# Linear attention and a two-level MoE on one core: a PSUM bank for the kv products, early rows turned by TensorE, and a new order of the steps

## The chip, the core and the metric

One core of a Trainium2 chip. Its engines run their own instruction streams: TensorE (PE; its weight loads are PEld), VectorE (DVE), ScalarE (ACT), GpSimd (POOL) and SyncE (SP, which here only issues DMAs). The metric is the device time of one execution in microseconds; the median of the runs counts.

## What is computed

Linear attention without softmax for 8 batches, 8 heads, 576 tokens and head size 64, an RMS norm over each head, then a mixture of experts: each of the 4,608 tokens picks one of 4 groups and one of 4 experts in it, and goes through that expert alone.

```python
kv  = einsum('bhsd,bhse->bhde', k, v)
out = einsum('bhsd,bhde->bhse', q, kv)
x   = out / sqrt(mean(out * out, -1) + 1e-6) * g_norm      # rows of 512 per token
g   = argmax(x @ w_group);  g_w = softmax(x @ w_group)[g]
e   = argmax(x @ w_expert[g]);  e_w = softmax(x @ w_expert[g])[e]
y   = g_w * e_w * (relu(x @ w1[g, e]) @ w2[g, e])
```

## The kernel before, in words

**Two phases.** The first does attention, routing and the sorting of the tokens by expert; the second runs the experts, one region of sorted rows after the other, the fullest first.

**Attention.** For each batch b, `kv_product` (L489, tiles `kps`) multiplies k and v, four products of two heads each. A chain of links makes `kvx` of it, kv beside kv times the router's weights: `kv_keep` copies it out of PSUM, `kv_transpose` turns it (L500, `tps`), `kvt_keep` copies (L504), `router_product` (L509, `eps_`), `router_keep`. All of them write the PSUM pool `ps_k`, which has one bank. Then `o_product` (L535, `ops`) gives a tile of 128 tokens, attention and logits in one product. There are 36 tiles: four for each batch, and one for the tails of each pair. For each tile `o_keep` (L540) copies to a ring `xo`, `logits_keep` copies the logits (`xr`), `squares` squares on ScalarE, or on POOL where SQUARE says G, and `mean_squares` sums on VectorE (L563, `ms`).

**Routing.** Tiles are routed in groups, GS = 7, 6, 6, 5, 6, 6. `route` finds for each token its expert and its weight on VectorE (L653 to L827), with a count over tokens on TensorE (L736 to L742, `rk`); `keys` (L768) are the rows in a DRAM buffer `xs`. There each pair of experts shares a stack that grows from the middle to both sides. For each tile POOL writes the factors (L835) and ids (L839) beside the rows and scatters them (`put_rows`, L244). After group PICK the fullest expert so far is picked (the star). After group EARLY, that is 24 tiles, its 256 outermost rows (HEAD) are read back by `early_region`: four DMAs by quarters of a row (L264) and one for the ids (L267). `scale_rows` (L281), `turn_x` (DVE transposes, L271) and ScalarE bring them into shape, and `early_products` puts them through the star's weights (L309, L313). This fills TensorE while the last group is routed. Then `order_regions` sorts the experts by count (`eidx`, `srow`).

**Order.** The steps of the first phase are not in the order of the code. Each `step` names an engine, a cost, the steps that it needs and a rank. `give_out` simulates the engines with these costs and emits the steps in the order that comes out; ties go by rank. The ranks (RANK, ROUTE, FOLD, LOADS, QLOADS, KVS) and costs are tables of numbers. Where the simulated TensorE would idle, `keep_warm` puts dummy products (L383, `warm`), one for each FILL = 0.28 us.

**Second phase.** `read(0)` reads the 128 rows of region 0 by quarters and `read(1)` those of region 1; after that SP loads the first full expert's weights (`load_weights`, L202). Region 0 goes through the star's weights in one piece (L309, L1367, L313). The last early product is cut in two (CUT), and region 0 is scaled and turned on VectorE between its halves. From region 1 on every product is done three times with split operands (L320, L321, L325), which holds TensorE for the rest of the time. Results are scattered to the output by POOL.

Of the kernel before, what the change touches and what calls it, by code (L numbers as in the profile page):

```python
# [24 lines left out]
GS = [7, 6, 6, 5, 6, 6]  # L25
XO = 20
XR = 18
QUICK = [0, 1, 2, 3, 4, 5]
# [3 lines left out]
EARLY = 3  # L32
# [3 lines left out]
RANK = {'ek': 1033.97, 'o': -457.88, 'ok': 58.4, 'sq': -33.02, 'red': -2582.62, 'w': -3332.77, 'wl': 4032.68, 'wl2': 4.61, 'xt': -3333.23, 'xs': -16.12, 'l1': -24.14, 'hs': -2608.76, 'l2': -2582.04, 'lk': -1004.47}  # L36
ROUTE = [-3190.17, 201.83, -3534.26, -636.71, 2427.37, -1191.6]
FOLD = [-6173.1, 4817.84, -3763.76, -4043.25, 6157.36, -6.99]
LOADS = [-9663.18, -8528.25, -2577.24, -29.38, 7.48, 419.99, 2424.36, 2902.19]
QLOADS = [-7229.2, -996.03, 2.08, -798.29, 41.64, 9.14, 962.0, 1915.11]  # L40
KVS = [-52.25, -5002.75, -4908.62, 59.57, -908.96, -793.37, 845.7, 4.08]
KEEP = 'DDAAAAAA'
SQUARE = 'AAGAAGAAGAAGAAGAAGAAGAAGA' + 'A' * 11
LOGITS = 'A' * 36
FILL = 0.28


SAME = {"PE": 0.0, "A": 0.14, "D": 0.14, "G": 0.1, "S": 0.0}
OTHER = {"PE": 0.2, "A": 0.16, "D": 0.18, "G": 0.1, "R": 0.0, "W": 1.2}
# [4 lines left out]
CUT = 5  # L54

@with_exitstack
def tile_linattn_moe(ctx: ExitStack, tc: tile.TileContext, qm, qt, k, v, router, w1, w2, out):
# [146 lines left out]

    def load_weights(expert):
        ev = expert_index(expert)
        parts = []
        for (wv, rows, cols) in ((w1v, DM, FF // 2), (w2v, FF, DM // 2)):
            for hf in range(2):
                t, d = load_half(ev, wv, rows, cols, hf)  # L210
                parts.append([t, None, None])
        return parts[0:2], parts[2:4]
# [43 lines left out]
    def read_quarters(x, row, n, eng, head=False):  # L256
        for i in range(4):
            cols = slice(REC * i, REC * (i + 1))
            for lo, hi in ((0, n // 32), (n // 32, n // 32 + 1)):
# [4 lines left out]
                got_rows(eng.dma_start(x[32 * i:32 * i + m, lo:hi, :], src.rearrange("(g t) f -> t g f", t=m)), head)  # L264

# [75 lines left out]
    sid = cp.tile([P, 2], I32, name="sid")  # L341
# [6 lines left out]
    with ExitStack() as ph:  # L348
# [4 lines left out]
        ps_e = ph.enter_context(tc.tile_pool(name="ps_e", bufs=2, space=bass.MemoryType.PSUM))  # L353
# [143 lines left out]
        def kv_transpose(b):  # L497
            kv["ps"] = ps_k.tile([P, 512], F32, name="tps", tag="psk")
            for pr in range(NP):
                nc.tensor.transpose(kv["ps"][:, pr * P:(pr + 1) * P], kvx[b % 4][:, pr, NR:NR + P], ident)  # L500

        def kvt_keep(b):
            kv["t"] = ap_.tile([P, 512], F32, name="kvt", bufs=1)
            nc.scalar.copy(out=kv["t"], in_=kv["ps"])  # L504
# [678 lines left out]
    with ExitStack() as ph:  # L1183
# [80 lines left out]
        def read(r):  # L1264
            row = first_row(srow[0:1, r:r + 1])
            read_quarters(xqs[r % 2], row, CAPS[r], nc.sync)
            if r == 0:
                read_ids(rid, row, 1, nc.sync)
# [316 lines left out]
```

## Time and profile before

| | us |
|---|---|
| median of 3 runs (565.05 to 567.49) | 566.06 |
| the profiled execution | 572.79 |
| its span, first to last instruction | 571.1 |
| PE busy in the span | 550.4 (96%) |
| DVE / ACT / POOL busy | 393.3 / 264.7 / 279.2 |
| HBM read and written | 106.04 MB and 20.58 MB |

Busy times are of the span. A busy TensorE isn't one that does useful work: the fillers count as busy too. In a timeline each row is a run of equal instructions: start, us, engine, line, operation, tiles and shapes; in brackets the idle time of the engine ahead of it and what ended that. In a view by windows each engine has its busy time and, in parentheses, its instructions; then come the granted clock of TensorE (1.00 is 2.4 GHz), the busy share of the DMA engines and GB/s.

### The profile page before, as it was taken

To read this page: it belongs to the slowest core of one execution; us is meant where nothing else is said; L and a number is where in the kernel's file an instruction comes from. 1 tells how busy PE (TensorE), PEld (TensorE's weight loads), DVE (VectorE), ACT (ScalarE), POOL (GpSimd) and SP (SyncE) were. 2 spreads that over 40 slices of the span, in tenths; PEclk is the share of its full clock that TensorE was granted. 3 is DMA by queue.
4 is the path that set the end of the run, shared out by engine and by line. 5 is a ranking of instruction groups with operands and counts; after the bars stand their busy time and mean duration, and the time that the engine had idled before them with its cause. 6 is when DMAs were issued, how large, how long until landed. Compare 5 with 4: busy or idle time off the path is not lost. (4 is left out here: it accounts for less than half of the span.)

```text
span 571.1 us, 11636 instructions
## 1 busy us (share of the span) xinstructions
PE 550.4 (96%) x4257; PEld 515.6 (90%) x4257; DVE 393.3 (69%) x777; ACT 264.7 (46%) x475; POOL 279.2 (49%) x314
## 2 busy tenths in 40 slices
PE   7999989999999999999999999999999997999995
PEld 3788877688599999999999999999999997999995
DVE  2347998861488677786768686777868785767760
ACT  0356665631355353445453544545454644455450
POOL 5012888463221381838383827355473834255181
PEclk9999999999999999999999999999999998999999
DMA  8999999435996545463846465564837473653010
GB/s 265 374 418 366 420 410 417 134 138 169 345 331 241 186 157 196 143 234 84 315 147 258 158 243 192 200 244 147 302 92 307 146 269 120 254 207 142 10 36 32
DMA packets 46126, 126.29 MB, mean 221 GB/s; under 512 B 7413, under 2 KB 28905, under 8 KB 35060
## 3 DMA queue, kind: packets, MB, share of 16 engines
q1 hardware_dynamic: 38132, 106.01, 51.6%
q0 software_dynamic: 7792, 19.48, 9.1%
q8 instruction: 34, 0.56, 0.4%
q10 hardware_dynamic: 144, 0.04, 0.1%
q14 instruction: 24, 0.20, 0.1%
HBM read 106.04 MB, written 20.58 MB: 222 GB/s over the span
## 5 line engine op out<-in xcount | busy, mean ns | idle before, releaser
L1305 POOL DMA_INDIRECT out_dram<-z,idx x141 | 168.5, 1195 | 177.8 <-DVE idx L1278 139.1
L320 PE MATMUL ps<-xh,whi 128*128 128x364 f32 (+14 forms) x480 | 144.1, 300 | 0.0
L325 PE MATMUL ps<-xh,wlo 128*128 128x364 f32 (+14 forms) x480 | 143.9, 300 | 0.0
L321 PE MATMUL ps<-xl,whi 128*128 128x364 f32 (+14 forms) x480 | 143.8, 299 | 0.0
L325 PE MATMUL psy<-hh,w2l 128*128 128x364 f32 (+13 forms) x448 | 136.0, 304 | 2.8 <-DVE w2l L298 2.2
L320 PE MATMUL psy<-hh,w2h 128*128 128x364 f32 (+13 forms) x448 | 135.7, 303 | 1.9 <-issue 1.9
L321 PE MATMUL psy<-hl,w2h 128*128 128x364 f32 (+13 forms) x448 | 136.1, 304 | 0.0
L228 DVE TENSOR_TENSOR wlo<-wr,whi 128x1024 fp32r<-128x1024 f32 x60 | 92.4, 1541 | 24.9 <-ACT whi L224 19.3
L284 ACT ACTIVATE hh<-ps 128x364 fp32r<-128x364 f32 (+14 forms) x120 | 50.3, 420 | 88.8 <-PE ps L325 66.3
L320 PEld LDWEIGHTS ps<-xh,whi 128*128 128x128 f32 x480 | 90.6, 189 | 0.0
L321 PEld LDWEIGHTS ps<-xl,whi 128*128 128x128 f32 x480 | 90.5, 189 | 0.0
L325 PEld LDWEIGHTS ps<-xh,wlo 128*128 128x128 f32 x480 | 90.5, 189 | 0.0
L325 PEld LDWEIGHTS psy<-hh,w2l 128*128 128x128 f32 x448 | 85.2, 190 | 3.9 <-DVE w2l L298 2.8
L320 PEld LDWEIGHTS psy<-hh,w2h 128*128 128x128 f32 x448 | 85.1, 190 | 2.2 <-issue 2.2
L298 DVE TENSOR_TENSOR w2l<-wr,w2h 128x1024 fp32r<-128x1024 f32 x60 | 74.6, 1243 | 17.5 <-ACT w2h L294 10.9
L321 PEld LDWEIGHTS psy<-hl,w2h 128*128 128x128 f32 x448 | 85.1, 190 | 0.3 <-DVE hl L285 0.2
L294 ACT CAST w2h<-wr 128x1024 fp32r<-128x1024 f32 x60 | 62.6, 1043 | 46.0 <-PE psy L321 46.0
L285 DVE SCALAR_TENSOR_TENSOR hl<-ps,hh 128x364 fp32r<-128x364 f32 (+14 forms) x120 | 55.5, 464 | 34.6 <-ACT hh L284 28.3
L1292 ACT ACTIVATE xh<-xt,rw 128x364 fp32r<-128x364 f32 (+14 forms) x60 | 32.7, 545 | 71.3 <-DVE xt L271 70.0
L224 ACT CAST whi<-wr 128x1024 fp32r<-128x1024 f32 x60 | 62.2, 1036 | 0.0
L281 POOL TENSOR_TENSOR xq<-xq 128x1280 f32<-128x1280 f32 (+4 forms) x15 | 35.5, 2367 | 22.3 <-DMA xq<-xs 22.2
L244 POOL DMA_INDIRECT xs<-xo,keys x36 | 38.0, 1056 | 13.2 <-POOL xo L839 7.1
(254 smaller groups left out, 653.5 us busy)
## 6 DMA issues: line engine op xcount, KB each, us to landing
wr<-in_w_dram SPq DMA_DIRECT2D x64, 1024.0 KB
m_q<-in_qm_dram SPq DMA_DIRECT2D x8, 1024.0 KB
m_k<-in_k_dram SPq DMA_DIRECT2D x7, 1024.0 KB
m_v<-in_v_dram SPq DMA_DIRECT2D x7, 1024.0 KB
xq<-xs SPq DMA_DIRECT2D x28, 136.0 KB
xq<-xs SPq DMA_DIRECT2D x20, 153.0 KB
out_dram<-z,idx POOLq DMA_INDIRECT x141
xq<-xs SPq DMA_DIRECT2D x8, 187.0 KB
```

The costliest lines, as they stand in the source:

```text
L224: nc.scalar.copy(out=hi, in_=w)
L228: eng.tensor_tensor(out=lo, in0=w, in1=hi.bitcast(F32), op=ALU.subtract)
L244: sc = nc.gpsimd.indirect_dma_start(out=xs, out_offset=bass.IndirectOffsetOnAxis(ap=keys[:, c:c + 1], axis=0), in_=x.rearrange("p i f -> p ...
L281: eng.tensor_tensor(out=part(x, n), in0=part(x, n), in1=factors(x, n), op=ALU.mult)
L284: nc.scalar.activation(out=hh, in_=ps, func=AF.Relu)
L285: nc.vector.scalar_tensor_tensor(out=hl, in0=ps, scalar=0.0, in1=hh.bitcast(F32), op0=ALU.max, op1=ALU.subtract)
L294: nc.scalar.copy(out=piece(hi, hf, i2), in_=halfpiece(wt[hf][0], i2))
L298: nc.vector.tensor_tensor(out=piece(lo, hf, i2), in0=halfpiece(wt[hf][0], i2), in1=piece(hi, hf, i2).bitcast(F32), op=ALU.subtract)
L320: nc.tensor.matmul(ps, lhsT=stat_h(c), rhs=mov_h(c), start=(c == 0), stop=False)
L321: nc.tensor.matmul(ps, lhsT=stat_h(c), rhs=mov_l(c), start=False, stop=False)
L325: nc.tensor.matmul(ps, lhsT=stat_l(d), rhs=mov_h(d), start=False, stop=(d == n - 1))
L1305: sc = nc.gpsimd.indirect_dma_start(out=out4, out_offset=bass.IndirectOffsetOnAxis(ap=idx[:, g:g + 1], axis=0), in_=z[:, g, :], in_offset= ...
```

## The change

- `kv_product` keeps the bank of `ps_k`; the other links of the chain and `rv` get a bank of their own, `ps_t`. `ps_e` falls from two banks to one, and the early products alternate between `ps_k` and `ps_e`.
- The star's rows, and those of region 0, are read whole, a token to a partition, by one DMA each (`read_tokens`), ids with them. `scale_tokens` scales and sorts the columns on VectorE, TensorE transposes, ScalarE copies out with the norm's gain. CUT is gone.
- The factors are written for a whole group by two VectorE operations; between two scatters POOL writes ids only. All squares are ScalarE's.
- The weighted logits lie with heads innermost (`pt`, `xr`).
- The two halves of w1 of the first full expert are loaded in the first phase (`next_weights`), w2 after `read(1)`.
- 7 groups, GS = 6, 5, 5, 4, 4, 6, 6; EARLY = 4 (again 24 tiles). Costs and ranks are new, so the order is too.

```diff
-GS = [7, 6, 6, 5, 6, 6]
+GS = [6, 5, 5, 4, 4, 6, 6]
-EARLY = 3
+EARLY = 4
-RANK = {'ek': 1033.97, 'o': -457.88, 'ok': 58.4, 'sq': -33.02, 'red': -2582.62, 'w': -3332.77, 'wl': 4032.68, 'wl2': 4.61, 'xt': -3333.23, 'xs': -16.12, 'l1': -24.14, 'hs': -2608.76, 'l2': -2582.04, 'lk': -1004.47}
+RANK = {'wn': 87.54, 'ek': -4236.76, 'o': 8245.9, 'ok': 5.78, 'sq': 116.73, 'red': 1698.88, 'w': -9.4, 'wl': 4910.9, 'wl2': -108.2, 'xt': -1910.07, 'xs': -38.32, 'l1': 16.82, 'hs': -2762.23, 'l2': 33.79, 'lk': -29.78}
...
-SQUARE = 'AAGAAGAAGAAGAAGAAGAAGAAGA' + 'A' * 11
+SQUARE = 'AAAAAAAAAAAAAAAAAAAAAAAAAAAAAAAAAAAA'
...
-OTHER = {"PE": 0.2, "A": 0.16, "D": 0.18, "G": 0.1, "R": 0.0, "W": 1.2}
+OTHER = {"PE": 0.2, "A": 0.27, "D": 0.18, "G": 0.1, "R": 0.0, "W": 1.2}
...
+    def read_tokens(x, row, nb, eng, head=False):
+        got_rows(eng.dma_start(x.rearrange("p j i f -> p j (i f)"),
+                               xs[bass.ds(row, P * nb), :].rearrange("(j p) f -> p j f", p=P)), head)
+
+    def scale_tokens(out, x):
+        nc.vector.tensor_tensor(out=out.rearrange("p (r i x) -> p i r x", r=4, i=4), in0=part(x, 4), in1=factors(x, 4),
+                                op=ALU.mult)
...
-        ps_e = ph.enter_context(tc.tile_pool(name="ps_e", bufs=2, space=bass.MemoryType.PSUM))
+        ps_t = ph.enter_context(tc.tile_pool(name="ps_t", bufs=1, space=bass.MemoryType.PSUM))
+        ps_e = ph.enter_context(tc.tile_pool(name="ps_e", bufs=1, space=bass.MemoryType.PSUM))
...
         def kv_transpose(b):
-            kv["ps"] = ps_k.tile([P, 512], F32, name="tps", tag="psk")
+            kv["e"] = ps_t.tile([P, 512], F32, name="tps", tag="pst")
...
         def router_product(b):
-            kv["ps"] = ps_k.tile([P, 512], F32, name="eps_", tag="psk")
+            kv["e"] = ps_t.tile([P, 512], F32, name="eps_", tag="pst")
...
-            xrt[c] = ap_.tile([P, H, NR], F32, name="xr", bufs=XR)
+            xrt[c] = ap_.tile([P, NR, H], F32, name="xr", bufs=XR)
...
+            def f():
+                for lo, hi in [(0, min(nt, XO - r0)), (min(nt, XO - r0), nt)]:
+                    for d in range(2 if hi > lo else 0):
+                        at = (r0 + lo) % XO
+                        eng.tensor_tensor(
+                            out=ring[:, at:at + hi - lo, d::2, FAC:FAC + 4],
+                            in0=v["rinv"][:, lo:hi].rearrange("p t (r h) -> p t h r", h=2),
+                            in1=v["cw"][:, lo:hi].unsqueeze(2).unsqueeze(3).to_broadcast([P, hi - lo, 2, 4]),
+                            op=ALU.mult)
+            w = do(e, nt * 16, [w], f, us=0.4)
+
             def put(c):
-                t = c - c0
-                nc.gpsimd.tensor_scalar(
-                    out=xot[c][:, :, FAC:FAC + 4].rearrange("p (h d) r -> p h d r", h=2),
-                    in0=v["rinv"][:, t, :].rearrange("p (r h) -> p h r", h=2).unsqueeze(2).to_broadcast([P, 2, 2, 4]),
-                    scalar1=v["cw"][:, t:t + 1], scalar2=None, op0=ALU.mult)
                 nc.gpsimd.tensor_copy(out=xot[c][:, :, TOK:REC].bitcast(I32),
...
         def early_region(do, rows):
...
-                row = first_row(star_row)
-                read_quarters(xq0, row, HEAD, nc.sync, head=True)
-                read_ids(sid, row, 2, nc.sync, head=True)
-            s = do("S", 0, rows + [done["star_row"]], f, us=4.7)
+                read_tokens(xq0, first_row(star_row), HEAD // P, nc.sync, head=True)
+            s = do("S", 0, rows + [done["star_row"]], f, us=2.8)
...
+        def next_weights():
+            def f():
+                st["next"] = expert_index(eidx[0:1, 1:2])
+                st["w1n"] = load_layer(st["next"], 0)
+            step("S", 5.1, RANK["wn"], [done["eidx"]], f, take=2)
...
+                    t["tr", j] = early_bank("xtr")
+                    for c in range(KC):
+                        nc.tensor.transpose(t["tr", j][:, c * P:(c + 1) * P], t["t"][:, j * DM + c * P:j * DM + (c + 1) * P],
+                                            ident)
...
-        w1n, w2n = load_weights(eidx[0:1, 1:2])
+        w1n, w2n = st["w1n"], load_layer(st["next"], 1)
...
-        whole2(o, h1, w2c[1], hi=CUT)
-        scale_rows(nc.vector, xqs[0], 4)
+        whole2(o, h1, w2c[1])
+        xn = xt.rearrange("p c t -> p (c t)")
+        scale_tokens(xn, xqs[0])
+        nc.scalar.copy(out=st["ys"][:, 1, DM // 2:DM], in_=o)
+        tp = ps_h.tile([P, 512], F32, name="ps")
         for c in range(KC):
-            turn_x(xt[:, c], xqs[0], 4, c)
-        nc.scalar.activation(out=xT, in_=xt, func=AF.Copy, scale=g2[:, 0:1])
-        whole2(o, h1, w2c[1], lo=CUT)
-        nc.scalar.copy(out=st["ys"][:, 1, DM // 2:DM], in_=o)
+            nc.tensor.transpose(tp[:, c * P:(c + 1) * P], xn[:, c * P:(c + 1) * P], ident)
+        nc.scalar.activation(out=xT, in_=tp.rearrange("p (c t) -> p c t", c=KC), func=AF.Copy, scale=g2[:, 0:1])
```

How the order moves is seen best at two places. The first is TensorE from batch 7's last kv product (`kps`) to its first tiles (`ops`). Before:

```order
L489 MATMUL kps<-tail_v,ktail_173 64x64 x2
...
L383 MATMUL warm<-wide_b,ones_b 128x512
L500 MATMUL tps<-ident,kvx_168 128x128 x4
...
L509 MATMUL eps__1565<-gw,kvt 128x40 x4
...
L535 MATMUL ops<-kvx_168,m_q 128x168 x8
```

and with the change, from the rank products of the group that ends with tile 24:

```order
L750 MATMUL rk<-ohs,upper_b 128x64
L543 MATMUL ops<-kvx_168,m_q 128x168 x4
L497 MATMUL kps<-m_v,m_k 64x64 x8
...
L497 MATMUL kps<-tail_v,ktail_175 64x64 x2
L543 MATMUL ops<-kvx_168,m_q 128x168 x4
L508 MATMUL tps<-ident,kvx_170 128x128 x4
...
L517 MATMUL eps__1554<-gw,kvt 128x40 x4
...
L543 MATMUL ops<-kvx_170,m_q 128x168 x12
```

A tile of the batch before (`kvx_168`) now stands where fillers stood between batch 7's products and their turning; three fillers are left on either side of `eps`.

The second place is SP's queue from the star's weights (`wr`) on. Before:

```order
L202 DMA wr_1348<-in_w_dram 128x2048
...
L202 DMA wr_1581<-in_w_dram 128x2048
L197 TENSOR_LOAD star_row
L264 ISA
L264 DMA xq_180<-xs 32x8x136
...
L267 DMA sid<-xs 128x2x1
L197 TENSOR_LOAD srow
L264 ISA
L264 DMA xq_1956<-xs 32x4x136
```

and with the change:

```order
L203 DMA wr_1567<-in_w_dram 128x2048
L198 TENSOR_LOAD star_row
L267 ISA
L267 DMA xq_182<-xs 128x2x544
...
L203 DMA wr_1767<-in_w_dram 128x2048
L194 TENSOR_LOAD eidx
L203 ISA
L203 DMA wr_1883<-in_w_dram 128x2048
L203 ISA
L203 DMA wr_1885<-in_w_dram 128x2048
L198 TENSOR_LOAD srow
L267 ISA
L267 DMA xq_1942<-xs 128x544
```

Three of the star's four weight loads now stand behind the head rows' read, and the next expert's two loads of w1 ahead of region 0's.

## Rows read from the trace of the kernel before

**Rows 1.** By windows: window and length, then PE, PEld, DVE, ACT, POOL, clock, DMA.
```profile
8.84:110.96 102.12, 95.57 (x1167) 79.85 (x1166) 70.96 (x213) 55.68 (x144) 46.93 (x81) 1.00 0.97 375
110.96:144.37 33.41, 33.27 (x160) 26.72 (x158) 16.58 (x74) 8.73 (x23) 17.10 (x28) 1.00 0.41 139
144.37:160.42 16.05, 15.32 (x57) 9.82 (x57) 8.08 (x12) 5.99 (x10) 3.79 (x2) 1.00 1.00 325
160.42:571.10 410.68, 399.63 (x2858) 396.65 (x2856) 294.31 (x467) 193.00 (x298) 204.14 (x158) 0.99 0.52 186
```
**Rows 2.** By windows, the filler products (`warm`) alone.
```profile
8.84:110.96 102.12, 17.74 (x66) 1.00 0.97 375
110.96:115.07 4.11, 4.11 (x19) 1.00 0.18 72
```
**Rows 3.** Who waited for whom, PE, 0 to 112 us: total, times, longest.
```profile
PE kps L489 <- DMA tail_v<-in_v_dram: 2.0, 3, 0.8
PE kps L489 <- DMA m_v<-in_v_dram: 1.7, 3, 0.8
```
**Rows 4.** Timeline of PE, from batch 7's last kv product to the early products.
```profile
98.08 0.64 PE L489 MATMUL kps<-m_v,m_k 128*64 128x64 f32 x16
98.55 0.29 PE L489 MATMUL kps<-tail_v,ktail 128*64 128x64 f32 x4
...
100.36 0.66 PE L500 MATMUL tps<-ident,kvx 128*128 128x128 f32 x4
...
108.93 0.47 PE L736 MATMUL rk<-carry,ones_f 1*128 1x112 f32 x2
...
109.66 1.36 PE L535 MATMUL ops<-kvx,tail_q 128*64 128x168 f32 x16
110.96 4.28 PE L383 MATMUL warm<-wide_b,ones_b 128*128 128x512 bf16 x19
115.07 8.80 PE L309 MATMUL l<-xx,wr 128*128 128x256 f32 x40
```
**Rows 5.** By windows, as in rows 1: the stretches in which attention's inputs load.
```profile
0.00:8.00 8.00, 5.80 (x19) 2.37 (x20) 3.33 (x12) 1.28 (x1) 7.13 (x46) 1.00 0.72 192
8.00:85.00 77.00, 70.76 (x915) 60.38 (x914) 48.42 (x127) 40.41 (x106) 30.32 (x51) 1.00 1.02 394
```
**Rows 6.** Timeline of POOL: one tile's scatter, the 24th's, and the last.
```profile
90.42 1.05 POOL L244 DMA_INDIRECT xs<-xo,keys  x1 [0.28 <-POOL xo L839]
91.51 0.36 POOL L835 TENSOR_SCALAR xo<-nwy,cw 128x16 f32<-128x16 f32 x1
...
92.30 1.05 POOL L244 DMA_INDIRECT xs<-xo,keys  x1 [0.28 <-POOL xo L839]
...
103.70 1.05 POOL L244 DMA_INDIRECT xs<-xo,keys  x1 [0.28 <-POOL xo L839]
...
132.34 0.97 POOL L244 DMA_INDIRECT xs<-xo,keys  x1 [0.30 <-issue]
```
**Rows 7.** Timeline of SP: the head rows' read, and region 0's.
```profile
106.72 2.35 SPq L264 DMA_DIRECT2D xq<-xs  x4
...
135.57 1.86 SPq L264 DMA_DIRECT2D xq<-xs  x4
```
**Rows 8.** Timeline of DVE: head rows scaled, last group's keys, region 0 scaled.
```profile
111.62 1.23 DVE L281 TENSOR_TENSOR xq<-xq 128x1024 f32<-128x1024 f32 x1 [0.42 <-DMA xq<-xs]
...
124.93 0.25 DVE L768 TENSOR_REDUCE keys<-kr 128x6 int32<-128x96 f32 x1
...
141.82 0.69 DVE L281 TENSOR_TENSOR xq<-xq 128x512 f32<-128x512 f32 x1 [0.35 <-DMA xq<-xs]
```
**Rows 9.** Timeline of ACT: a copy of 512 columns out of PSUM.
```profile
101.05 0.58 ACT L504 COPY kvt<-tps 128x512 f32<-128x512 f32 x1 [0.48 <-PE tps L500]
```
**Rows 10.** By windows, as in rows 1: a stretch of the second phase.
```profile
470.00:480.00 10.00, 6.94 (x54) 6.50 (x53) 4.72 (x7) 3.77 (x8) 8.03 (x7) 1.00 0.16 54
480.00:485.00 5.00, 4.29 (x23) 4.29 (x24) 3.72 (x7) 2.81 (x4) 0.00 (x0) 0.66 0.68 234
```

More of the change, by code (lines that the diff above doesn't have):

```diff
@@ L203, in load_half, with load_layer @@
         return t, d
+    def load_layer(ev, layer):
+        wv, rows, cols = ((w1v, DM, FF // 2), (w2v, FF, DM // 2))[layer]
+        return [[load_half(ev, wv, rows, cols, hf)[0], None, None] for hf in range(2)]
     def load_weights(expert):
         ev = expert_index(expert)
[L207 to L212, printed above, removed]
+        return load_layer(ev, 0), load_layer(ev, 1)
     def quarter(part, h):
@@ L1060, in f @@
                 nc.vector.tensor_copy(out=eidx, in_=v["rv"][0:1, 0:NE])
[L1061 removed]
+            y = done["eidx"] = do("D", 16, [x], f)
             def f():
@@ L1119, in early_products, with early_bank, f @@
             t = {}
-            x, free = [], [None, None]
-            for c in range(KC):
-                def f(c=c):
-                    if c == 0:
-                        t["tx"] = big.tile([P, 2, KC, HEAD], F32, name="xx", tag="w8")
-                        t["t"], t["x"] = t["tx"][:, 0], t["tx"][:, 1]
-                    turn_x(t["t"][:, c], st["xq0"], HEAD // 32, c)
-                s = step("D", 0.35, r0 + RANK["xt"] + 0.1 * c, st["scaled"], f, take=1 if c == 0 else 0)
-                def f(c=c):
-                    nc.scalar.activation(out=t["x"][:, c], in_=t["t"][:, c], func=AF.Copy, scale=g2[:, 0:1])
-                x.append(step("A", 0.35, r0 + RANK["xs"] + 0.1 * c, [s], f))
+            x = []
+            bank = [0]
+            def early_bank(nm):
+                bank[0] += 1
+                return (ps_k, ps_e)[(bank[0] - 1) % 2].tile([P, 512], F32, name=nm, tag=("psk", "pse")[(bank[0] - 1) % 2])
+            free = [done["kk", B - 1], None]
+            for j in range(HEAD // P):
+                def f(j=j):
+                    if j == 0:
+                        t["tx"] = big.tile([P, 2, KC, HEAD], F32, name="xx", tag="w8")
+                        t["t"], t["x"] = t["tx"][:, 0].rearrange("p c t -> p (c t)"), t["tx"][:, 1]
+                    scale_tokens(t["t"][:, j * DM:(j + 1) * DM], st["xq0"][:, j])
+                s = step("D", 0.62, r0 + RANK["xt"] + 0.1 * j, [st["read"]], f, take=1 if j == 0 else 0)
+                def f(j=j):
+                    if j == 1:
+                        st["warm"] = None
+                    t["tr", j] = early_bank("xtr")
+                    for c in range(KC):
+                        nc.tensor.transpose(t["tr", j][:, c * P:(c + 1) * P], t["t"][:, j * DM + c * P:j * DM + (c + 1) * P],
+                                            ident)
+                s = step("PE", 0.62, r0 + RANK["l1"] - 1 + 0.1 * j, [s, free.pop(0)], f)
+                def f(j=j):
+                    nc.scalar.activation(out=t["x"][:, :, j * P:(j + 1) * P],
+                                         in_=t["tr", j].rearrange("p (c t) -> p c t", c=KC), func=AF.Copy,
+                                         scale=g2[:, 0:1])
+                x.append(step("A", 0.59, r0 + RANK["xs"] + 0.1 * j, [s], f))
+                free.append(x[-1])
             hs = []
@@ L1134, in f @@
                 def f(f_=f_):
-                    st["warm"] = None
-                    t["l1", f_] = ps = ps_e.tile([P, 512], F32, name="l1", tag="pse")
+                    t["l1", f_] = ps = early_bank("l1")
                     whole1(ps[:, 0:HEAD], st["ws"][f_ // 4][:, :, f_ % 4 * P:(f_ % 4 + 1) * P], t["x"])
```

100 lines of the change are left out of this document (50 added, 50 removed).

## The prediction

> **What bounds the kernel now.** I read the windows first: they cut the execution where TensorE's work changes [rows 1]. From 160.42 us to the end TensorE is busy 399.63 of 410.68 us with products that this change leaves as they are, so nothing is to be won there. From 110.96 to 160.42 us it is busy too. The room is ahead of 110.96 us, the end of the last attention tile's product: 95.57 of 102.12 us count as busy, but part of that is the `warm` filler. The filler alone stands in the next view [rows 2]: 19 fillers follow each other in 4.11 us, so one takes 0.216 us of TensorE's time. The stretch from 8.84 to 110.96 us holds 64 of them whole (two of the 66 only reach into it), 13.8 us. Real work is 95.57 - 13.8 = 81.8 us, and 6.55 us is idle. Most of that idle time ends with a load of k or v: 2.0 and 1.7 us [rows 3]. The other engines are not full: VectorE is busy 70.96 and ScalarE 55.68 of the 102.12 us [rows 1]. The DMA is: 0.97 of its engines' time there.
>
> Why fillers are there is read from the timeline [rows 4]. The products of batch 7 end at 98.84, then come fillers, the turning of its kv (100.36) and fillers again: TensorE waits for ScalarE and VectorE at each link of the chain from a batch's kv to its first tile. All links of that chain write one PSUM bank, so the next batch's products cannot be put between them.
>
> **The change, part by part.** *Own bank and new order.* In the new order 25 fillers stand between the first kv product and the last tile's product instead of 64, because tiles and kv products of another batch stand between the links. That takes away 39 x 0.216 = 8.4 us. A seventh group adds one more set of rank products, 0.7 us (108.93 to 109.66 [rows 4]). So TensorE's own time says: the attention ends at 8.84 + 81.8 + 5.4 + 0.7 = 96.7 us if no wait is left, and at 103.3 us if all 6.55 us of waits stay. The DMA gives a second floor. Up to 85 us it moves 1.5 + 30.3 = 31.8 MB [rows 5]. The loads up to batch 7's v are 27.0 MB (28.3 MB of inputs less one q and its tail), and some 18 scatters of 0.279 MB stand among them, 5.0 MB. So this v lands at about 85.4 us. Four products of at most 0.76 us (98.08 to 98.84) and the 12.1 us from 98.84 to 110.96, less four fillers that are gone there (0.9 us), end the attention at 99.6 us. The early expert's weights did not compete with this before, as they were issued last; three quarters of them now come behind the head rows. I take 102: the load waits (3.7 us) stay and half of the other 2.8 us too. The ends 96.7 and 103.3 go into the range.
>
> *Head rows* (256 rows of the most wanted expert). These can only be read when the scatters of 24 tiles have landed. POOL is late with them: one tile takes 1.88 us (90.42 to 92.30), and the 24th is out at 104.75 [rows 6]. The factors (0.36 us a tile) go to VectorE as two operations a group, so a tile falls to 1.52 us, and the squares of the tiles up to here leave POOL for ScalarE, which has room [rows 1]. POOL is then not behind when the 24th tile's keys come, just ahead of batch 7's products (say 86.5 us): four tiles end at 92.6, the read starts 1.97 us later as before (106.72 after 104.75 [rows 7]), at 94.6, and lands within the 4.9 us that it took before (VectorE starts at 111.62 [rows 8]), at 99.5 us. That is ahead of 102, so one DMA for five is hidden and counts nothing. If this slack of 2.5 us is gone, the start of the early products slips one for one. The three weight loads behind the read take 2.7 us each at the 394 GB/s of rows 5 and are in by 110 us. The second half of w1 is wanted after four blocks of 1.76 us (five in 8.80 [rows 4]), later than that.
>
> *Early rows turned by TensorE.* Before, 4.11 us passed from the last tile to the early products. Now: 4 fillers (0.9), eight transposes (0.66 for four [rows 4], 1.3), a copy by ScalarE (0.58 [rows 9]) with about 0.1 of handing over: 2.9 us. The early products last as before, 115.07 to 144.37, 29.3 us. Then region 0 is turned by TensorE too, and the filling of that gap with part of the last early product is dropped: 0.66 for the transposes and 0.7 for the copy, in which TensorE stands still. Sum from the last tile to region 0's products: 2.9 + 29.3 + 1.4 = 33.6 us, 0.2 more than the 33.41 of before [rows 1].
>
> *What hides the last group's route.* Counted from the last tile, its keys were done after 14.2 us (125.18), the last scatter after 22.4 (133.31), the first region read started after 24.6 and its rows came after 30.9 (141.82) [rows 6 to 8]. TensorE now wants them, scaled in 0.69, 32.2 us after the last tile. So they are 0.6 us early even without the gain from one DMA for five and from the unit stride of the logits' sum, which I therefore price at nothing. *Two loads of w1* for the next expert now stand ahead of this read on SP's queue. They take 5.3 us and may start while POOL scatters for 8.1 us (125.18 to 133.31). If their slots came late, up to 5.3 us would fall on the read. Between 144.37 and 160.42 us these two loads are gone from a DMA that is at 1.00 there; TensorE idles only 0.73 us in it, so I take nothing.
>
> *The clock.* Through the whole attention the granted clock is 1.00, the 2.4 GHz level, with 6.55 us of idle time in it. Fillers hold TensorE busy while it waits, and most are taken out. The Trainium skill's page TensorE: Matmul & The Clock Gate (What's actually happening) says that "the default state is throttled, and activity releases the throttle", which speaks against taking fillers out. By that rule a stage whose waits are longer than planned would run slow; the trace agrees in so far as no fall is seen where fillers stand, and no run here shows the stage without them.
>
> **Sum.** Attention end 110.96 to 102: -9.0. From there to region 0: +0.2. After it: 0. So -8.8 us. The profiled execution took 572.79 us (span 571.10), 6.7 us over the median of 566.06; TensorE lost time in it at 470 to 485 us (6.94 busy of 10, then a clock of 0.66 [rows 10]), far behind everything that changes. So I take the difference off the median: 557.3 us.
>
> **Rivals.** *Fillers were only a symptom.* Loads or VectorE pace the attention, each filler removed turns into a wait, and its end stays at 111. For it: the DMA share of 0.97. Against it: the bytes, which allow 99.6. Time: 566.06 + 0.2 = 566.3 us.
>
> *Head rows come as late as before.* The attention ends at 102, but POOL or the route holds the read at 106.72; it lands at 109.5 to 111.6, and scaling, turning and copying bring the early products to about 113.2 instead of 115.07. Region 0 costs its 1.4 us more. Time: 566.06 - 1.9 + 1.4 = 565.6 us. For it: the 11 us by which POOL trailed. Against it: 0.36 of 1.88 us a tile is gone.
>
> *The clock falls* (the other side). Where batches 5 to 7 are processed, about 57 to 99 us, 9 fillers are left. If waits for loads grow there and the clock goes to the 1.2 GHz level, work takes twice as long. If half of some 40 us of work runs so: 566.06 - 8.8 + 20 = 577 us. It decides from 8.8 + 2.8 = 11.6 us of such work on. For it: the 0.66 that followed a stretch of 6.94 busy in 10 [rows 10]. Against it: waits of up to 2 us in sum [rows 3] left the clock alone.
>
> **How the numbers follow.** A measurement of this kernel can tell about 0.5%, 2.8 us, from no change. The forecast has a chance of 0.74; with attention ends from 96.7 to 106 it gives 552 to 561 us. Fillers as a symptom: 0.10. Late head rows: 0.08. The clock: 0.08. The first is faster, the middle two are no change, the last is slower. The range reaches from the lower floor to the late head rows, 552 to 566, and leaves out the other two.
>
> **What would show it.** In the changed profile: the last tile's product ending at 100 to 104 us, some 25 fillers ahead of it, POOL's tiles at 1.5 us each, the head read starting ahead of 97 us, the early products less than 4 us behind the last tile, about 1.4 us between the last early product and region 0's, and 33 to 34 us from the last tile to region 0. I am wrong if the attention ends after 107, if a granted clock under 1.00 stands ahead of 150 us, or if region 0 waits for its rows.

## The result and the profile after

The changed kernel took 560.44 us (median of 4 runs, 558.91 to 560.96) beside 566.73 us of the kernel before: a ratio of 0.9889, with a 95% interval from 0.9857 to 0.992. That is 6.3 us less; the forecast was 557.3 us, 8.8 less, with a range of 552 to 566. The profiled execution took 560.28 us. (Ratios leave disturbed runs out and medians do not, so that the two can differ, as in experiment 2.)

By windows, cut at the same places of the program as [rows 1] (columns as there): the attention to the last tile's product, the early products, region 0, the rest.

```profile
9.46:101.63 92.17, 85.82 (x1131) 76.28 (x1130) 62.81 (x245) 60.08 (x155) 29.34 (x48) 1.00 0.97 376
101.63:138.67 37.04, 33.90 (x158) 27.58 (x156) 14.53 (x67) 8.75 (x22) 14.94 (x21) 0.95 0.76 270
138.67:155.20 16.53, 15.31 (x57) 9.82 (x57) 8.08 (x12) 5.72 (x9) 3.78 (x2) 1.00 0.90 279
155.20:558.60 403.40, 396.62 (x2858) 395.05 (x2856) 293.71 (x467) 193.30 (x298) 203.92 (x158) 1.00 0.52 186
```

The attention ends 9.33 us earlier (101.63 for 110.96). The second window is 3.6 us longer, at a mean granted clock of 0.95, and the third 0.5 longer. The rest takes 403.4 us, and 403.3 to 403.9 in the profiles of experiments 5 to 11 and of the control run: so the start of region 1 tells the time of a profiled execution. For the kernel before, 160.42 + 403.6 + 1.7 around the span gives 565.7 us, near its medians of 566.7 here and 565.6 to 566.4 on the second chip of the experiments. Its own profiled execution took some 7 us more for the rest, most of it where the prediction said [rows 10].

The fillers alone, as in [rows 2], in the attention:

```profile
9.46:101.63 92.17, 6.82 (x27) 1.00 0.97 376
```

27 where 66 were (some only reach into the window). Who waited for whom on PE, 9.46 to 165 us (total, times, longest), as in [rows 3]; the first line is one of the kernel before, the others are of the changed kernel:

```profile
PE ops L535 <- DMA m_q<-in_qm_dram: 0.4, 1, 0.4
...
PE ops L543 <- DMA m_q<-in_qm_dram: 2.8, 3, 1.4
PE kps L497 <- DMA m_v<-in_v_dram: 1.9, 3, 1.1
PE kps L497 <- DMA tail_v<-in_v_dram: 1.4, 2, 0.7
PE xtr L1157 <- DVE xx L271: 1.3, 1, 1.3
PE ps L317 <- ACT xT L1386: 0.9, 1, 0.9
PE l L317 <- ACT xx L1162: 0.8, 1, 0.8
```

In the attention, waits for loads make up nearly all idle time: 6.1 of 92.17 - 85.82 = 6.35 us, where they were 4.1 of 6.55 before. New are the waits of the handover, as this text calls the stretch from the last attention tile to the early products. The timeline of PE (as [rows 4]) shows them:

```profile
100.33 1.36 PE L543 MATMUL ops<-kvx,tail_q 128*64 128x168 f32 x16
101.63 1.04 PE L391 MATMUL warm<-wide_b,ones_b 128*128 128x512 bf16 x4
103.92 1.32 PE L1157 MATMUL xtr<-ident,xx 128*128 128x128 f32 x8 [1.25 <-DVE xx L271]
106.02 10.59 PE L317 MATMUL l<-xx,wr 128*128 128x256 f32 x40 [0.78 <-ACT xx L1162]
...
137.13 0.63 PE L1385 MATMUL ps<-ident,xT 128*128 128x128 f32 x4 [0.17 <-PE ps L321]
138.67 0.70 PE L317 MATMUL ps<-wr,xT 128*128 128x512 f32 x1 [0.90 <-ACT xT L1386]
```

From the last tile to the early products 4.39 us pass instead of the 2.9 of the forecast, and the first five blocks take 10.59 us instead of 8.80. The windows show why; the last columns are the granted clock, the DMA share and GB/s:

```profile
101.60:106.00 4.40, 2.35 (x14) 1.15 (x12) 2.76 (x7) 2.87 (x7) 1.83 (x3) 1.00 1.04 428
106.00:108.00 2.00, 1.98 (x5) 1.61 (x6) 1.36 (x6) 0.47 (x2) 1.72 (x3) 0.53 1.07 389
108.00:110.00 2.00, 2.00 (x8) 1.57 (x7) 1.95 (x5) 0.27 (x1) 1.72 (x3) 0.62 1.00 255
110.00:112.00 2.00, 2.00 (x11) 1.77 (x10) 1.77 (x7) 0.50 (x2) 1.50 (x4) 1.00 0.92 351
```

TensorE was busy 2.35 of 4.40 us, then ran for 4 us near the 1.2 GHz level.

Two reads come late, seen on POOL (24th and last scatter) and SP (head read, region 0's), as in [rows 6, 7]:

```profile
93.80 1.00 POOL L244 DMA_INDIRECT xs<-xo,keys  x1 [0.28 <-POOL xo L855]
...
125.08 0.97 POOL L244 DMA_INDIRECT xs<-xo,keys  x1 [0.30 <-issue]
```

```profile
99.40 0.39 SPq L267 DMA_DIRECT2D xq<-xs  x1
100.08 23.22 SPq L203 DMA_DIRECT2D wr<-in_w_dram  x5
133.08 0.33 SPq L267 DMA_DIRECT2D xq<-xs  x1
```

The head read is issued 4.6 us after the 24th scatter left POOL (94.80), and region 0's 7.0 us after the last (126.05). Before, these were 1.97 and 2.3 us [rows 6, 7]. What lies between is in the DMA queues (packets, MB, share of the engines), from 126 to 128, 128 to 130 and 130 to 133 us; hardware_dynamic carries SP's loads, here w1 of the next expert, software_dynamic POOL's scatters:

```profile
q1 hardware_dynamic: 95, 0.65, 88.3%
q0 software_dynamic: 15, 0.07, 7.9%
```

```profile
q1 hardware_dynamic: 70, 0.57, 82.2%
q0 software_dynamic: 66, 0.22, 27.2%
```

```profile
q0 software_dynamic: 159, 0.55, 44.7%
q1 hardware_dynamic: 32, 0.13, 10.8%
```

POOL has issued its last scatter, but while the loads run, little of the scatters moves; most of it comes after 130 us, and only then can the read go out. The Trainium skill's page DMA: Bandwidth & Descriptors (Queues, rings and completion order) says that each DMA engine takes turns between the queues, packet by packet. The 70 and 66 packets from 128 to 130 us agree with it; the 95 and 15 before do not show such turns, and the profile does not tell how many of the scatters' packets were ready then.

**Theory.** The attention is shorter as forecast; 2.5 us of the gain go to loads ahead of two reads in the DMA: the star's first load ahead of the head rows, the next expert's w1 ahead of region 0's. **Rivals.** The reads wait for something else (memory, registers); the clock at the handover is what costs; and, for the gain, bank, fillers or factors.

### The profile page after: what moved, and what is told of

Same layout as the page of the kernel before. It is cut to its first block, busy times and chain, and to the rows that moved or that the text cites. A ratio compares the mean times of both kernels' runs of the same rounds, so it can differ in the third digit from the quotient of the medians.

```text
span 558.6 us, 11537 instructions
## 1 busy us (share of the span) xinstructions
PE 538.9 (96%) x4218; PEld 511.5 (92%) x4218; DVE 382.2 (68%) x803; ACT 269.1 (48%) x484; POOL 259.4 (46%) x276
## 3 DMA queue, kind: packets, MB, share of 16 engines
q1 hardware_dynamic: 36468, 106.01, 53.1%
## 5 line engine op out<-in xcount | busy, mean ns | idle before, releaser
L244 POOL DMA_INDIRECT xs<-xo,keys x36 | 36.1, 1003 | 74.8 <-ACT y L670 41.4
```

What stands on the lines that cost most here:

```text
L244: sc = nc.gpsimd.indirect_dma_start(out=xs, out_offset=bass.IndirectOffsetOnAxis(ap=keys[:, c:c + 1], axis=0), in_=x.rearrange("p i f -> p ...
```

## The experiments

Experiments 1 to 4 ran on one chip, all others on another. Ratios are to the kernel before on the same chip; on the second chip it took 566.43 us beside the control and experiments 5 to 7, and 565.55 beside 8 to 11. Milestones are from one profile each, in us; the attention's end is the last tile product's start plus 1.30. The changed kernel and the control are the same code, and their milestones lie up to 1.6 us apart: so far can two profiles of one kernel differ.

| | attention end | early products | region 0 | region 1 | median | ratio (95%) |
|---|---|---|---|---|---|---|
| before | 110.96 | 115.07 | 144.37 | 160.42 | 566.73 | 1 |
| forecast | 102 | 104.9 | 135.6 | 151.6 | 557.3 | |
| changed | 101.63 | 106.02 | 138.67 | 155.20 | 560.44 | 0.9889 (0.9857 to 0.992) |
| control | 101.30 | 105.46 | 137.08 | 154.21 | 560.2 | 0.9896 (0.9863 to 0.9929) |
| 5 one bank | 102.67 | 110.88 | 141.60 | 157.40 | 563.43 | 0.9953 (0.9927 to 0.9979) |
| 6 no fillers | 103.27 | 106.01 | 137.91 | 155.11 | 558.19 | 0.9871 (0.9831 to 0.9912) |
| 7 factors on POOL | 109.24 | 117.00 | 147.72 | 163.52 | 570.43 | 1.006 (1.0034 to 1.0086) |
| 8 both loads late | 101.26 | 104.02 | 134.77 | 150.57 | 556.36 | 0.9849 (0.9819 to 0.9878) |
| 9 and covered | 101.95 | 105.87 | 137.27 | 153.07 | 555.43 | 0.9815 (0.9789 to 0.9841) |
| 10 one bank, pinned | 101.44 | 105.86 | 136.59 | 155.38 | 559.2 | 0.9883 (0.9855 to 0.9911) |
| 11 head by quarters | 102.47 | 107.39 | 138.13 | 153.94 | 558.2 | 0.9865 (0.9837 to 0.9892) |

**1. The next expert's w1 behind the reads.**

```diff
         early_products(early_weights())
-        next_weights()
...
-        w1n, w2n = st["w1n"], load_layer(st["next"], 1)
+        w1n, w2n = load_weights(eidx[0:1, 1:2])
```

> The changed kernel with one thing undone: the two loads of the next expert's w1 stand behind the reads of regions 0 and 1 on SP's queue again. In the changed kernel the last scatter left POOL at 126.05 us, these loads kept the DMA busy from about 121 to 131.8, and the read of region 0 was issued at 133.08 only. Theory: the scatters land behind those 2 MB. Then the read is issued some 2 us after the last put, near 128, and the rows are there near 131.5. As the early products end at 137 in any case, that is worth 0.2 to 0.5 us: region 0's products at 138.2 to 138.5 instead of 138.67, time -0.5 to 0 us against the changed kernel. Rival: the read waits for memory that the first phase frees (TensorE or ScalarE), not for the scatters; then it stays near 133. Second rival: the loads are needed early; then region 1's first product comes later and the time rises by 1 to 5 us.

**2. The star's first load behind the head read.**

```diff
-                               [wt[-1] if wt else None, done["star_idx"]], f,
+                               [wt[-1] if wt else st["read"], done["star_idx"]], f,
```

> The changed kernel with the first load of the star's weights (1 MB) behind the read of the head rows instead of ahead of it. In the changed kernel the 24th scatter left POOL at 94.80, the read was issued at 99.40, 4.6 us later instead of 1.97 in the kernel before. Theory: that scatter landed behind loads still in the DMA, this MB among them (2.5 us at 410 GB/s). Then the read is issued near 97, VectorE scales near 100.5 to 101, TensorE turns right after the last tile, and the early products start at 103.5 to 104.5 instead of 106.02, at a granted clock of 1.00 instead of 0.53 to 0.62. Region 0's rows then bound the rest, as the next expert's loads still hold their read back: 2 to 4 us faster than the changed kernel. Rival: the read waits for something else (SP's register loads, the star's index) and stays at 99.4: no change, or slower by up to 2.5 us because the weights come later.

**3. Both edits.**

> Both edits: the star's first load behind the head read and the next expert's w1 behind the reads of regions 0 and 1. Theory: early products start at 103.5 to 104.5, clock 1.00, region 0's rows near 128 to 129 and no longer a bound; region 0's products 3.5 to 4.5 us ahead of the changed kernel's 138.67, so 3.5 to 4.5 us faster than it, some 556.5 us, and at least 1 us faster than with the star's load alone if region 0's rows were the bound there. Rival: the last group's route is the next bound (TensorE waits at its rank products, up to 2 us): 2 us faster than the changed kernel only.

**4. The edit of 1, and fillers in the handover.**

```diff
+                    if j == 0:
+                        for _ in range(6):
+                            nc.tensor.matmul(st["warm"], lhsT=ones_b, rhs=wide_b, start=True, stop=True)
...
+                    if f_ == 0:
+                        hold = ps_t.tile([P, 512], F32, name="hold", tag="pst")
+                        for _ in range(4):
+                            nc.tensor.matmul(hold, lhsT=ones_b, rhs=wide_b, start=True, stop=True)
```

> The next expert's w1 behind the reads, the star's load left as in the changed kernel, and fillers in the two gaps of the handover: six more ahead of the early rows' transposes and four between these and the first early product (0.216 us each, 2.2 us in gaps of 1.25 and 0.78 us plus what stands beside). Theory: the clock of 0.53 to 0.62 from 106 to 110 us followed from these gaps; with them filled it stays at 1.00, the five early blocks take 8.8 us instead of 10.6, and the time falls by 1.5 to 1.8 us against the kernel with the loads alone moved, if the fillers themselves cost nothing, by 1.2 if they overhang. Rival: the clock falls there for another reason; then the blocks keep 10.6 us and the time is the same or 0.3 us longer.

Measured: 574.74, 577.29, 576.97 and 575.85 us; ratios 1.01 (1.0061 to 1.0139), 1.0005 (0.9955 to 1.0056), 1.011 (1.0065 to 1.0154) and 1.0086 (1.0044 to 1.0128). All times missed what I expected, by a cause that none of the edits touches: the attention ended at 119.6, 120.6, 121.6 and 115.8 us. The table of PE's waits of experiment 3, 9 to 120 us:

```profile
PE tps L508 <- ACT kvx L486: 5.3, 2, 3.9
PE kps L497 <- issue: 3.0, 8, 0.4
```

Inside the products of k and v TensorE stands still for 0.4 us at a time with no releaser in the profile ("issue"), and ScalarE's copy of such products into `kvx` starts 4.2 us after the last of them has ended (56.94 to 61.15; in experiment 8, the same code on the other chip, 0.03 us after):

```profile
56.63 0.31 PE L497 MATMUL kps<-tail_v,ktail 128*64 128x64 f32 x2 [0.38 <-issue]
...
61.15 0.74 ACT L486 COPY kvx<-kps 64x256 f32<-64x256 f32 x2 [7.14 <-PE ops L543]
```

One part can be read all the same, since it hangs on the last scatters alone (experiment 8 has more profiles for it). With the w1 loads in place (2) region 0's read went out 7.0 us after the last scatter had left POOL (140.32 to 147.36); with them behind (1 and 3) 2.3 us after (140.75 to 143.06, 141.25 to 143.56). So the read waits for the scatters to land, and they land behind the loads; that it waits for memory is out. Experiment 4 tells nothing of the clock: the five blocks took 8.90 us with the gaps filled, and 8.90 in experiment 1 with a gap of 0.92 left.

**Control. The changed kernel again.**

> The changed kernel itself, without an edit, on the chip that the other three share. In the first four experiments TensorE stood still for some 0.4 us at a time inside the products of k and v (53 to 57 and 80 to 86 us), with no semaphore or load behind it, ScalarE once for 5.4 us near 86, and the attention ended near 119 to 121 us instead of 101.6. If that belongs to the chip or to how instructions reach the engines there, this kernel shows it too: about 574 us, 1% slower than the kernel before. If it came from the edits, this kernel shows none of it: attention end near 101.6, 560.4 us, 0.989 of the kernel before.

(The "other three" are experiments 5 to 7.)

On the second chip nothing stood still: 560.2 us, as first measured. PE's timeline:

```profile
103.36 1.32 PE L1157 MATMUL xtr<-ident,xx 128*128 128x128 f32 x8 [1.03 <-DVE xx L271]
105.46 8.90 PE L317 MATMUL l<-xx,wr 128*128 128x256 f32 x40 [0.78 <-ACT xx L1162]
...
135.55 0.63 PE L1385 MATMUL ps<-ident,xT 128*128 128x128 f32 x4 [0.83 <-PE ps L321]
```

The gaps are nearly those of the first profile (1.03 and 0.78 us), yet the five blocks take 8.90 us at a clock of 1.00. The 1.7 us saved do not all arrive: TensorE now waits 0.83 us ahead of region 0's transposes, as that read still went out at 131.52 only, and region 1 starts 1.0 us earlier.

**5. One bank for the whole chain.**

```diff
-            kv["e"] = ps_t.tile([P, 512], F32, name="tps", tag="pst")
+            kv["e"] = ps_k.tile([P, 512], F32, name="tps", tag="psk")
...
-                prev = get("kk", b - 1)
+                prev = get("ek", b - 1)
```

(and the same for `eps_` and for the early products' first bank).

> The changed kernel with the links of the kv chain back in the bank of the kv products, and the next batch's products held until the chain is through; order found by the same table of ranks. 33 fillers stand between the first kv product and the last tile instead of 25. Theory (the bank is what lets other work stand between the links): about 8 x 0.28 us of planned idle time more and real waits with it, attention end 2 to 4 us later, time 2 to 4 us above the changed kernel. Rival (the new order and costs brought the gain, the bank little): within 1 us of it.

+3.2 us, as the theory had it, but not by its mechanism: the attention ended only 1.4 us later, and that was the clock. Behind a wait for a load of q, 16 products of tiles took 4.19 us; 2.52 in the changed kernel, at a clock of 1.00. PE's timeline:

```profile
19.80 4.19 PE L543 MATMUL ops<-kvx,m_q 128*128 128x168 f32 x16 [1.14 <-DMA m_q<-in_qm_dram]
```

and the window, in which the clock is 0.67:

```profile
20.00:25.00 5.00, 5.00 (x52) 4.82 (x53) 0.69 (x1) 2.34 (x6) 0.00 (x0) 0.67 1.03 389
```

Six of its twelve runs, with a mean clock of 0.988 to 0.990, took 564.0 to 566.8 us; the other six, at 0.995 to 0.998, took 561.1 to 562.9. The planner also put three of the star's loads ahead of the head read, which was issued at 104.13, 6.1 us after the 24th scatter had left POOL. So this one is confounded; experiment 10 repeats it without that.

**6. No fillers** (`FILL = 1000.0`).

> The changed kernel without any filler. Theory: its 25 fillers in the attention (5.4 us) stand in waits that are there anyway, so the attention ends where it did or up to 1 us earlier if the clock stays; but a granted clock under 1.00 already followed gaps of 1.25 and 0.78 us at the handover to the early products, so stretches after the unfilled waits should run at it: 1 to 8 us slower than the changed kernel. Rival (fillers don't hold the clock): clock 1.00 as before in the attention, time the same or up to 1 us less.

558.19 us, no loss. The granted clock fell once, behind a wait of 2.19 us for a load of q (0.97 over 50 to 100 us):

```profile
70.00:75.00 5.00, 2.83 (x10) 2.86 (x11) 3.65 (x16) 1.57 (x4) 3.89 (x8) 0.71 1.03 421
```

The attention ended 2.0 us later than in the control, the early products started only 0.6 us later (106.01): VectorE scales the head rows from 103.23, with no idle time behind the last tiles' sums, where it had idled 1.3 us ahead of them in the control.

**7. The factors back on POOL.**

```diff
             def put(c):
+                if not last:
+                    t = c - c0
+                    nc.gpsimd.tensor_scalar(out=xot[c][:, :, FAC:FAC + 4].rearrange("p (h d) r -> p h d r", h=2),
...
```

> The changed kernel with the factors back on POOL, one operation a tile ahead of each scatter (all groups but the last). Theory: a tile costs POOL about 0.36 us more, 1.9 instead of 1.5; the eight tiles that POOL puts in a row ahead of the head read (83.0 to 94.8 us) end 2 to 3 us later, the head read and the early products slip by as much, 2 to 3 us slower than the changed kernel. Rival (the head read is held by loads in the DMA, not by POOL): the read is issued at the same time and the loss stays under 1 us.

10.2 us slower than the control, far more than expected. VectorE's timeline:

```profile
80.54 0.19 DVE L678 SCALAR_TENSOR_TENSOR nwa<-nwa,m 128x32 f32<-128x32 f32 x1
86.44 0.19 DVE L683 SCALAR_TENSOR_TENSOR nwy<-nwa,y 128x32 f32<-128x32 f32 x1 [5.71 <-POOL xo L858]
```

and PE's windows (the clock is the third number from the end):

```profile
85.00:90.00 5.00, 0.69 (x2) 0.69 (x3) 3.49 (x10) 0.85 (x2) 4.12 (x7) 0.79 1.01 419
90.00:95.00 5.00, 5.00 (x24) 4.45 (x23) 2.72 (x13) 2.43 (x7) 0.47 (x2) 0.53 1.02 423
```

`nwy` is one buffer for all groups, and POOL's factors read it between the scatters. VectorE may not write the next group's norms until POOL is through (9.0 us in two such waits), ScalarE waits behind VectorE, TensorE behind both, and then its clock falls to 0.53. In the kernel before, POOL's factors read one such buffer too, and the table of VectorE's waits (8 to 112 us) has no wait for it: the price belongs to the new order. That the buffer is all of the 10.2 us is not shown: a second buffer was not tried, and the order moved with the costs. (Three star loads stood ahead of the head read here, which went out 2.0 us after the 24th scatter left POOL at 104.96.)

**8. Both loads late, on the second chip.** The kernel of experiment 3, unchanged.

> The same kernel as in the third experiment (star's first load behind the head read, next expert's w1 behind the reads of regions 0 and 1), once more, as the changed kernel showed none of the stalls of the first four experiments on another chip. If the stalls belong to the chip: attention end near 101.5, head read issued near 97, early products from 103.5 to 104.5, the read of region 0 some 2 us after the last put, region 0's products from 134 to 135 (changed kernel 138.67 in its first profile, 137.08 in its second), 2.5 to 4 us faster than the changed kernel's 560.2, which stood at 0.9896 of the kernel before. If the stalls came with the edits, or the chip is the first one again: attention end near 120 and about 1% slower than the kernel before.

As expected: 556.36 us, 3.8 less than the control (2.7 by the ratios, whose intervals just overlap). From POOL's and SP's timelines:

```profile
93.42 1.00 POOL L244 DMA_INDIRECT xs<-xo,keys  x1 [0.28 <-POOL xo L855]
...
120.10 0.97 POOL L244 DMA_INDIRECT xs<-xo,keys  x1 [0.31 <-ACT h L1177]
```

```profile
97.11 0.40 SPq L267 DMA_DIRECT2D xq<-xs  x1
...
123.38 0.33 SPq L267 DMA_DIRECT2D xq<-xs  x1
```

2.7 and 2.3 us instead of 4.6 and 7.0. All profiles agree on region 0's read: it went out 6.0 to 7.9 us behind the last scatter in the eight with the w1 loads ahead of it, and 2.3 in the six without, the kernel before among them. The star's load holds its read only where the scatter is early: with it 4.5 to 4.7 us pass from scatters that left POOL at 94.3 to 95.5 (control, changed, 11), but 2.0 us from those at 96.3 and 96.8 (6 and 10). Against the control the early products start 1.4 us earlier, region 0 2.3 and region 1 3.6: by these two profiles the star's load is worth 1.4, region 0's rows 0.9, and region 1's rows, whose read follows region 0's on SP's queue, 1.3. For the last of these, ScalarE's timeline of the changed kernel:

```profile
145.87 0.60 ACT L1328 ACTIVATE xh<-xt,rw 128x364 fp32r<-128x364 f32 x1 [1.15 <-DVE xt L279]
146.37 0.58 ACT L1411 ACTIVATE hr<-ps 128x512 f32<-128x512 f32 x1
```

Region 0's second `hr` stands behind a piece of region 1 (`xh`) that waits for its rows, and TensorE waits for `hr`: 0.77 us there, 1.35 in the control, 0.3 here. And experiment 3 and this one are the same code: 1.011 on one chip, 0.9849 on the other.

**9. And region 0 covered.** As 8, with this:

```diff
-        whole2(o, h1, w2c[1])
+        whole2(o, h1, w2c[1], hi=6)
...
+        whole2(o, h1, w2c[1], lo=6)
```

(scaling and transposes between the two, the clearing of `psy` behind them).

> As the first of this call, and the last early product cut in two again (six of its eight pieces, then the four transposes of region 0, then two pieces), with region 0 scaled on VectorE ahead of the clearing of the second phase's banks. Theory: the transposes' copy by ScalarE (0.9 us in which TensorE waits) and the waits for rows lie beside the last two pieces (0.9 us), as region 0's rows come some 5 us earlier than in the changed kernel: 0.8 to 1.5 us faster than the first of this call. Rival: the rows come later than TensorE reaches the transposes, which then hold the last pieces up: same time or up to 1 us slower.

("The first" is experiment 8.)

555.43 us, the fastest median, 0.9 below experiment 8; the two intervals overlap, so the step itself is likely, not shown. In its profile the cover works, and another edge shows:

```profile
105.87 8.83 PE L317 MATMUL l<-xx,wr 128*128 128x256 f32 x32 [1.96 <-DMA wr<-in_w_dram]
...
135.77 0.60 PE L1379 MATMUL ps<-ident,xT 128*128 128x128 f32 x4
136.21 1.03 PE L321 MATMUL ps<-wr,h 128*128 128x256 f32 x4
137.27 0.70 PE L317 MATMUL ps<-wr,xT 128*128 128x512 f32 x1
```

No wait is left ahead of region 0. But in this execution (558.31 us, the longest of its six) the star's load, now behind the head read, came 1.96 us late, and after that gap the clock was 0.77 and 0.50 from 106 to 110 us: four blocks in 8.83 us, 7.17 in experiment 8.

**10. One bank, pinned.** As 5, and the star's second load waits for the head read.

> One bank for the whole kv chain as in the fifth experiment, but with only one of the star's loads ahead of the head read, as in the changed kernel; there, three stood ahead of it and the read was issued at 104.13 instead of 98.79 us. Theory: the bank's own price is what the attention's end showed, 102.9 instead of 101.3 us, so 1 to 2 us above the changed kernel (ratio to the kernel before 0.991 to 0.993), and the rest of the 3.2 us was the late head read. Rival: the whole 3.2 us is the bank's, and stays (0.995).

559.2 us, nothing lost: 0.9883 beside the control's 0.9896. The attention ends at 101.44; the price that the theory had taken from experiment 5 was the clock's. (Region 1 starts 1.2 us behind the control's, which is no more than two profiles of one kernel differ by.) In PE's timeline tiles stand between the links, with the one bank:

```profile
65.11 0.60 PE L508 MATMUL tps<-ident,kvx 128*128 128x128 f32 x4
65.55 1.31 PE L543 MATMUL ops<-kvx,m_q 128*128 128x168 f32 x8
66.69 0.98 PE L517 MATMUL eps__1037<-gw,kvt 128*128 128x40 f32 x8
```

**11. The head rows by quarters, turned by VectorE** (the four reads, the read of the ids, `scale_rows` and `turn_x` of the kernel before).

> The changed kernel with the head rows read by quarters in five DMAs and turned by VectorE as in the kernel before (region 0 stays with TensorE). Theory: five issues and a turn of both blocks by VectorE make the early products start 1.2 to 2 us later (from the head read's issue to the first early product 9.3 us before, 6.6 to 6.7 in the changed kernel), of which region 0's own wait for its rows takes up to 0.8: 0.4 to 2 us slower than the changed kernel. Rival (nothing hangs on it, one DMA is hidden): the same time within 0.4 us.

The early products start at 107.39, 1.9 us later, as expected; but then nothing waits for region 0's or region 1's rows, and region 1 starts at 153.94, 0.3 us earlier. 558.2 us: no loss. Region 0's read went out at 131.22, as in the control (131.52), so its rows set the pace in both; with the loads moved as in 8 the quarters were not tried.

## Why the prediction was right, and where it was not

**The attention's end** (forecast 102, floors 96.7 and 103.3): 101.63. The mechanism held, fewer fillers and load waits that stay, but that the end came so close is in part luck: three terms were off, and they offset each other. TensorE's busy time fell by 9.75 us (95.57 to 85.82), where the sum had 8.4 - 0.7 = 7.7. I had priced a filler at the 0.216 us that it takes in a long run; the busy time of the fillers alone fell from 17.74 to 6.82 us, 10.9 instead of 8.4. Against that, 6.35 us of idle time stayed, where I had kept 5.1 of 6.55, and the stretch began 0.6 us later (9.46 for 8.84).

**Its reason was wrong in part.** I wrote that all links of the chain write one bank, "so the next batch's products cannot be put between them". True, but tiles can: experiment 10 has the one bank, 34 fillers in its trace (27 with two banks, 66 before), and the same time within the noise. Nor do the fillers matter for the time (6), though without them the attention ended 2.0 us later. The factors on VectorE I priced as 0.36 us of POOL a tile; with them back on POOL the new order loses 10.2 us (7), and the trace shows VectorE waiting for a buffer that POOL still reads. As the kernel before has no such wait, this is what the new order needs, not what it won. How much of the 9.3 us came from the factors, from the squares or from the order itself, no run here separates: the order was not tried on the kernel before, and the cause of the gain stays open among these.

**Head rows, "hidden by 2.5 us".** This step failed. The read went out at 99.40 instead of 94.6. Of these 4.8 us 2.2 are POOL's: the 24th scatter left it at 94.80 instead of 92.6, because the keys were done at 87.40, not 86.5, and POOL was busy with the group before until 88.40. The other 2.6 us are the way from the scatter to the read. I carried 1.97 us from scatter to read over from a place where the DMA share was 0.17 (104 to 105 us in the trace of before); the changed kernel does it at 0.94 (94 to 96 us), behind the one star load that the new order leaves ahead of the read and that I gave no price. The handover took 4.39 us (control 4.16) instead of 2.9. It slipped as the prediction said that it would if the slack was gone.

**Early products, 29.3 us.** 29.26 in the control; 30.9 in the first profile, 1.7 of it the clock at the handover. That is the clock rival in small, at a place that I had not named. What followed from it was 1 us, not 20.

**"Two loads of w1": up to 5.3 us, taken at nothing.** The mechanism was in the text and the price was wrong. The read came 7.0 us behind the last scatter; of that, region 0 felt 0.2 to 0.8 us, and region 1's start 1.3 more, through a queue on ScalarE that I had not looked at. "After it: 0" failed in this place alone; from region 1 on the profiles lie within 0.6 us of each other, and the kernel before, by its median, with them.

**The sum.** Region 1 was to start at 151.6. The control has 154.21: attention -0.7, handover +1.3, early products to region 0 +0.9, region 0 to region 1 +1.1, which is the 2.6 us missing. With both loads moved (8) region 1 starts at 150.57 and the time is 0.9849 of before, where the forecast was 557.3 / 566.06 = 0.9845.

**Rivals.** "Only a symptom" and "as late as before" are out: the attention ended 9.3 us earlier, and the head read went out 7.3 us earlier.

**Signs.** Three came as written: the last tile's end, some 25 fillers, POOL's tiles at 1.5 us. Four did not: the head read was not ahead of 97 us (99.40), the early products were 4.39 us behind the last tile, 1.7 us lay ahead of region 0's products, and 37.0 us passed from the last tile to region 0. Of the three signs of being wrong two appeared: the clock under 1.00, and region 0 waiting for its rows (0.17 us, 0.83 in the control). So the attention was forecast well, and what lies between it and region 1 was not.

## What to carry to other kernels

Here a read that waits for scatters was as late as the loads queued ahead of it: put big loads behind it, even where they look free, and take the delay from issue to landing at the DMA's load of the place, not from a quiet place. Count idle time to see what can be won, but undo a part at a time before saying what won it: here bank and fillers, the visible parts, could be undone at no loss, and putting one small POOL operation back cost 10 us. Read the granted clock by windows before giving a microsecond to an edit: in experiment 5 it was the clock's. The part of the program that comes behind the change, constant at 403.6 us, turns every profile into a measurement of the change in that one execution.

## What the runs showed of the hardware

**The clock.** At the handover, gaps of 1.25 and 0.78 us were followed by a granted clock of 0.53 in the changed kernel's first profile; gaps of 1.03 and 0.78 us in the control, and of 1.98 and 0.78 in experiment 5, by 1.00. Early in the attention, waits of 1.08 and 1.14 us were followed by 0.67 in experiment 5, and waits of 1.09 and 0.98 us at the same places by 1.00 in the changed kernel. After single stops of 2.19 us (6), 4.84 (7) and 1.96 (9) it fell to 0.71, 0.53 and 0.50. The Trainium skill's page TensorE: Matmul & The Clock Gate (What's actually happening) says that activity releases the throttle; 6, 7 and 9 agree, the handover of experiment 5 does not show it, and what decides in such short gaps stays open. Experiment 6 is the attention without fillers, which no trace had shown ahead of the prediction: one fall, and no longer time.

**Instructions that come late.** On one chip TensorE stood still 0.4 us at a time in its densest stretch of small products, with the DMA share at 1.00 to 1.01, and ScalarE started a copy 4.2 us after its input was there; the same code on another chip did not (single stops of 0.4 us stand in 5 and 10). The kernel before took 569.8 and 565.6 to 566.4 us on the two chips, so it suffered less. Why was not settled: the changed kernel itself was not run beside the first four, and no run lowered the DMA's load there. Until then the gain of 1.1% is that of the chips on which it was measured.
